# Row maxima of the scale chains in one VectorE operation with an accumulator, with another order of the work

## The chip, the core and the metric

The kernel runs on one core of a Trainium2 chip. Its engines work beside each other, each through its own stream of instructions in program order: TensorE multiplies matrices, VectorE, ScalarE and GpSimd work on elements, and DMA queues move data. An instruction that waits holds everything behind it on its engine. The metric is the device time of one execution in microseconds, the median of three runs.

## The reference

Three stages follow each other, in float32; the first weights arrive as float64.

```python
scores = scale * q @ k.T                      # 2 batches, 8 heads, 576 tokens, 64 wide
# heads 0-3: a local band of 32 positions; heads 4-7: every 32nd position
attn = exp(scores - max) / sum
x = attn @ v                                  # 1152 tokens x 512
h = maximum(maximum(x @ w1, x @ w2), x @ w3)  # 512 x 768 each
x2 = h @ w_out                                # 768 x 512
for e in range(4):                            # p: the normalised domain_probs
    out += p[:, e:e+1] * (maximum(x2 @ we1[e], 0) @ we2[e])
```

The experts are 512 x 1024 and 1024 x 512.

## The kernel before

**Split numbers.** Every product of the dense stages is made from fp16 pairs: an operand is scaled by a power of two, and split into hi (ScalarE, `split`) and lo (VectorE, the rest); three matmuls per piece give hi·hi + hi·lo + lo·hi (`mm3`, lines 350 to 352). The scale comes from a chain for each operand: a maximum per partition (VectorE `absmax`, line 132), or a bound by a sum (ScalarE `sum_bound`, line 129); if there are several, a reduction of them (line 95); a small matmul that lays all partitions' values beside each other in PSUM, `rows` (line 98); then on VectorE a maximum over these 128 columns (line 100), the guard and the factor (`m`, line 111, or line 119 for float64 words), a bit operation that keeps the exponent (line 114 or 122) and a reciprocal (`s`, line 105). There are 21 such chains: 4 for v, 6 for groups of w1 to w3, 1 for w_out, 2 for x2, and 4 each for the experts' two weight matrices.

**Tiling.** Tokens go in four groups i (two batches, halves of 256 and 320). Attention takes each group in four head pairs p, two local and two strided: scores and exponentials (`att_a`, the atom aa; score blocks are `sps`, lines 259 and 264, in two PSUM buffers; the exponentials are line 275), normalisation (an; the multiplication on GpSimd, line 298), transposition (at), product with v (ap, `ops`; the result is split into x, lines 344 and 345). The columns of w1 to w3 come in six groups fc of 128: load lw, maximum wa, decoding of float64 words wd (ScalarE lines 162 and 163, VectorE 166 and 167), split wp. `g1` (atom g) multiplies one token group by one column group for all three weights, into three PSUM tiles out of a pool of three; the first is copied out by ScalarE (line 396), the other two are joined by VectorE (397, 398). `g2` (atom go) multiplies by w_out into the same pool; ScalarE copies to `x2acc` (line 418) and VectorE takes the maximum. The experts' first product runs as seven products over sums and differences of blocks (lines 564 to 566), whose operands `prep_w1` (atom ew) and `x2_ops` (xw, yw) make; `gemm1` adds the products up on VectorE (572 to 579) and splits the hidden values (588 and 589, or 585 and 586 with GpSimd).

**Order.** The table ORDER lists the atoms of everything up to the first expert in the order in which the code issues them; XS, W20, W10, W2S and W1S say how many steps of the preparation for later products go between the experts' products. A scheduler then sets each engine's stream by its own model of time, so a moved atom changes more than its own place. In ORDER, oa, od, os and op are the maximum, decoding, scale and split of w_out; ew are steps of the first expert's weight preparation.

Of the kernel before, what the change touches and what calls it, by code (L numbers as in the profile page):

```python
# [8 lines left out]
F32 = mybir.dt.float32  # L9
# [5 lines left out]
ALU = mybir.AluOpType  # L15
# [14 lines left out]
QB = 3  # L30
XS = [0, 1, 1]
W20 = [2, 1, 3, 2, 0, 5, 1, 2]
W10 = [1, 1, 2, 2, 4, 4, 0, 3]
W2S = [0, 0, 1, 0, 1, 1, 4, 6, 3, 0, 7, 5, 7, 3, 1, 3, 1]
W1S = [8, 3, 1, 2, 0, 14, 6, 6, 4, 0, 4, 4, 0, 5, 0, 3, 3]

ORDER = """
    lq02 lq00 lq01 aa00 lw0 lv01 lq03 lv00 aa01 vs0 wa0 wd0 an00 lq20 at00 ap00 lw1 aa02 lv21 wp0 an01 at01
    ap01 an02 lq22 aa03 an03 at02 lv20 ap02 at03 lq21 lq23 ap03 aa20 vs2 lq10 aa21 wa1 an20 at20 wd1 ap20 lq12
    aa22 g00 lw3 an21 at21 aa23 ap21 wp1 an22 lw2 lv11 at22 ap22 an23 g01 at23 lv10 lq11 ap23 wd2 wa2 wa3 wd3  # L40
    wp3 aa11 wp2 g20 lq32 g21 lv30 an11 g03 aa10 g23 aa12 vs1 lw4 at11 ap11 an10 at10 ap10 lq30 wa4 wd4 lq13
    wp4 g04 g02 an12 lv31 aa13 at12 ap12 lw5 wa5 an13 at13 wd5 lq33 wp5 aa30 an30 ap13 lo0 lq31 aa33 aa31 vs3
    g22 lo1 g24 at30 ap30 an31 at31 an33 oa1 at33 ap31 ap33 aa32 an32 oa0 at32 g25 od0 od1 ap32 os op3 op0 g10
    op4 fo ew g05 op1 op2 ew ew op5 go20 ew go00 ew go23 ew ew g11 ew ew go22 ew g12 go21 ew go01 ew go03 ew
    go02 ew xw g15 xw g13 fw g14 ew xw xw g30 g31 xw g32 xw fw g33 ew xw xw ew xw g34 fw fw fw g35 cl go10 m
    go11 go30 fw m go13 fw go12 go31 go32 go33 m yw yw yw yw yw yw yw yw m yw fw
"""
# [6 lines left out]
def kernel(ctx, tc, qk0l, qk0s, qk1l, qk1s, vl, vs0, vs1, vn, masks, w123, wo, probs, we1, we2, out):  # L54
    nc = tc.nc
# [33 lines left out]

    def all_max(maxes, n):  # L90
        red, eye = maxes, ident if maxes.dtype == F32 else identb
        if n > 1:

            red, eye = sc.tile([128, 1], BF16, tag="red", name=nm("red")), identb
            nc.vector.tensor_reduce(red, maxes, AX.X if len(maxes.shape) == 2 else AX.XY, ALU.max)

        rows = rows_tile()
        nc.tensor.matmul(rows, red.to_broadcast([128, 128]), eye, start=True, stop=True)
        allr = sc.tile([128, 1], F32, tag="allr", name=nm("allr"))
        nc.vector.tensor_reduce(allr, rows, AX.X, ALU.max)  # L100
        return allr

# [5 lines left out]
    def scale_of(maxes, n, inv=None, f=0.25):  # L108

        m = sc.tile([128, 1], F32, tag="m", name=nm("m"))  # L110
        nc.vector.tensor_scalar(m, all_max(maxes, n), TINY, f, ALU.max, ALU.mult)
        if inv is None:
            inv = const.tile([128, 1], F32, name=nm("inv"))
        nc.vector.tensor_scalar(inv.bitcast(I32), m.bitcast(I32), 0x7F800000, None, ALU.bitwise_and)
        return finish_scale(inv)

    def scale_of64(maxes, n, inv=None):
        m = sc.tile([128, 1], F32, tag="m", name=nm("m"))
        nc.vector.tensor_scalar(m, all_max(maxes, n), REBIAS, TINY64, ALU.mult, ALU.max)
        if inv is None:  # L120
# [338 lines left out]
    def x2_ops(j, pool):  # L459
# [7 lines left out]
        (nc.gpsimd if j else nc.vector).tensor_tensor(t[2], a[0][0], a[1][0], ALU.subtract)  # L467
        nc.vector.tensor_tensor(t[3], a[0][1], t[1], ALU.subtract)
        yield
# [83 lines left out]
    def gemm1(e, j):  # L553
# [3 lines left out]
        for fp in range(4):  # L557
# [22 lines left out]
            for b in range(2):  # L580
                tok = slice(n * b, n * b + n)
                hi, lo = [hh[:, i, :, tok].rearrange("p (a f) t -> p a f t", f=4)[:, :, fp, :] for i in range(2)]
                if b and (e or j):
                    nc.scalar.activation(c[:, b], c[:, b], AF.Relu)
# [272 lines left out]
```

## Time and profile before

| | us |
|---|---|
| median of three runs (575.19 to 577.38) | 576.4 |
| the profiled execution | 576.38 |
| its span in the trace | 574.6 |
| TensorE busy (matmuls) | 551.3 |
| VectorE busy | 364.6 |
| ScalarE busy | 264.4 |
| GpSimd busy | 127.9 |

In the rows below the engines are PE (TensorE), PEld (its weight loads), DVE (VectorE), ACT (ScalarE) and POOL (GpSimd). A row gives the line of the kernel, the operation, and the tiles written and read; the brackets or the last column give the time for which the engine had been idle just before, and which engine's work ended that. The busy share over the whole span hides that the stages differ, so the windows come first.

### The profile page before, as it was taken

What the parts mean: (1) busy time and instruction counts of PE and PEld (TensorE: products, weight loads), DVE (VectorE), ACT (ScalarE), POOL (GpSimd) and SP (SyncE); (2) the same over time, 40 slices, a digit from 0 to 9 for tenths busy, and PEclk for the clock granted to TensorE, in tenths of its full rate; (3) what the DMA queues carried; (4) which work ended last, traced back from release to release, by engine and by line L of the source; (5) the groups of instructions that cost most, each with busy time, mean ns of one, the idle gap of its engine ahead of it and who ended that gap; (6) DMA issues with size and microseconds to landing.
All of it is one profiled execution on the core that took longest, in us unless ns stands there. A gap on an engine that the chain in (4) does not pass through costs nothing.

```text
span 574.6 us, 9788 instructions
## 1 busy us (share of the span) xinstructions
PE 551.3 (96%) x3944; PEld 373.6 (65%) x3944; DVE 364.6 (63%) x676; ACT 264.4 (46%) x559; POOL 127.9 (22%) x115
## 2 busy tenths in 40 slices
PE   5789699999999999899999999999999999999997
PEld 3668588887877777674447875446875446875443
DVE  3888999687652254988864765984764943765111
ACT  4678877586541132567826443605433611433000
POOL 1233554310111101023504211260211200221000
PEclk9588999999999999999999999999999999999999
DMA  8999636000400003004260000340000000000111
GB/s 291 337 352 306 206 115 256 2 2 2 147 1 1 1 2 141 6 1 148 73 220 0 1 2 1 128 165 1 2 1 1 1 0 1 2 1 0 56 55 56
DMA packets 16109, 44.33 MB, mean 77 GB/s; under 512 B 2280, under 2 KB 2280, under 8 KB 15296
## 3 DMA queue, kind: packets, MB, share of 16 engines
q1 hardware_dynamic: 15920, 43.41, 22.6%
q8 instruction: 31, 0.51, 0.4%
q10 hardware_dynamic: 144, 0.30, 0.1%
q14 instruction: 14, 0.11, 0.1%
HBM read 41.34 MB, written 2.36 MB: 76 GB/s over the span
## 4 chain that ended last, share of the span: by engine, by line
PE 77%; DVE 8%; DMA 6%; ACT 5%; issue 3%; POOL 1%; SPq 0%; ACTq 0%; DVEq 0%; POOLq 0%
PE e L350 11%; PE e L352 11%; PE e L351 11%; PE w L564 9%; PE w L566 9%; PE w L565 8%; PE g L350 6%; PE g L351 6%; PE g L352 6%; DMA v<-in_vl_dram 2%; DMA st<-in_w_dram 2%; ACT w L129 1%; PE ops L337 1%; DMA st<-in_we_dram 1%; ACT p L275 1%
## 5 line engine op out<-in xcount | busy, mean ns | idle before, releaser
L565 PE MATMUL w<-xops,w1ops 128*128 128x256 f16 (+1 forms) x448 | 128.0, 286 | 0.7 <-DVE xops L473 0.7
L564 PE MATMUL w<-xops,w1ops 128*128 128x256 f16 (+1 forms) x448 | 127.4, 286 | 1.0 <-DVE c L573 0.6
L566 PE MATMUL w<-xops,w1ops 128*128 128x256 f16 (+1 forms) x448 | 128.0, 286 | 0.0
L351 PE MATMUL g<-x,w 128*128 128x256 f16 (+1 forms) x288 | 82.4, 288 | 0.0
L350 PE MATMUL g<-x,w 128*128 128x256 f16 (+1 forms) x288 | 81.6, 289 | 0.2 <-ACT t L396 0.2
L352 PE MATMUL g<-x,w 128*128 128x256 f16 (+1 forms) x288 | 81.8, 286 | 0.0
L586 POOL TENSOR_TENSOR h<-c,h 128x640 f16<-128x640 f32 (+1 forms) x28 | 36.5, 1304 | 186.4 <-ACT h L585 182.1
L694 DVE SCALAR_TENSOR_TENSOR x2acc<-e,coef,x2acc 128x512 f32<-128x512 f32 x27 | 20.1, 747 | 69.5 <-PE e L352 69.5
L588 ACT ACTIVATE h<-c 128x512 f16<-128x512 f32 (+1 forms) x36 | 24.1, 676 | 83.0 <-DVE c L578 82.8
L351 PE MATMUL e<-st,h 128*128 128x512 f16 x144 | 54.6, 379 | 0.0
L352 PE MATMUL e<-w,h 128*128 128x512 f16 x144 | 54.6, 379 | 0.0
L350 PE MATMUL e<-st,h 128*128 128x512 f16 x144 | 54.6, 379 | 0.0
L352 PE MATMUL e<-st,h 128*128 128x512 f16 x144 | 54.6, 379 | 0.0
L351 PE MATMUL e<-w,h 128*128 128x512 f16 x144 | 54.4, 379 | 0.0
L350 PE MATMUL e<-w,h 128*128 128x512 f16 x144 | 54.0, 379 | 0.0
L565 PEld LDWEIGHTS <-w1ops 128*128 128x128 f16 x448 | 43.8, 98 | 13.4 <-issue 1.6
L566 PEld LDWEIGHTS <-w1ops 128*128 128x128 f16 x448 | 43.8, 98 | 12.6 <-issue 1.7
L564 PEld LDWEIGHTS <-w1ops 128*128 128x128 f16 x448 | 43.8, 98 | 12.0 <-DVE c L577 0.2
L352 PEld LDWEIGHTS <-h 128*128 128x128 f16 x288 | 28.2, 98 | 34.0
L350 PEld LDWEIGHTS <-h 128*128 128x128 f16 x288 | 28.2, 98 | 33.0
L351 PEld LDWEIGHTS <-h 128*128 128x128 f16 x288 | 28.2, 98 | 32.7
L400 POOL TENSOR_TENSOR h<-t,h 128x256 f16<-128x256 f32 (+1 forms) x24 | 21.9, 918 | 89.4 <-ACT h L399 89.4
(133 smaller groups left out, 1028.7 us busy)
## 6 DMA issues: line engine op xcount, KB each, us to landing
st<-in_we_dram SPq DMA_DIRECT2D x16, 1024.0 KB, 5.2
st<-in_w_dram SPq DMA_DIRECT2D x6, 1536.0 KB, 11.2
st<-in_wo_dram SPq DMA_DIRECT2D x2, 1536.0 KB, 8.4
qk<-in_qk1s_dram SPq DMA_DIRECT2D x4, 684.0 KB, 11.5
out_dram<-x2acc SPq DMA_DIRECT2D x8, 256.0 KB, 2.0
qk<-in_qk1l_dram SPq DMA_DIRECT2D x4, 496.0 KB, 11.3
qk<-in_qk0l_dram SPq DMA_DIRECT2D x4, 400.0 KB, 12.2
qk<-in_qk0s_dram SPq DMA_DIRECT2D x4, 384.0 KB, 12.9
```

Source lines behind the costliest of these rows:

```text
L129: nc.scalar.activation(junk, src, AF.Abs, scale=2.0**-12, accum_out=dst)
L275: nc.scalar.activation(p3[:, g, :], s3[:, j, :], AF.Exp, bias=ngm[:rows, g : g + 1], scale=0.125, accum_out=sm[:rows, g : g + 1],)
L350: nc.tensor.matmul(psum, lh, rh, start=i == 0, stop=False)
L351: nc.tensor.matmul(psum, lh, rl, start=False, stop=False)
L352: nc.tensor.matmul(psum, ll, rh, start=False, stop=i == n - 1)
L400: nc.gpsimd.tensor_tensor(hh[:, 1, fc, :], t1[:, :n], hh[:, 0, fc, :], ALU.subtract)
L564: nc.tensor.matmul(pt, wh, xh, start=k == 0, stop=False)
L565: nc.tensor.matmul(pt, wh, xl, start=False, stop=False)
L566: nc.tensor.matmul(pt, wl, xh, start=False, stop=k == 1)
L586: nc.gpsimd.tensor_tensor(lo, c[:, b], hi, ALU.subtract)
L588: nc.scalar.activation(hi, c[:, b], AF.Relu)
L694: nc.vector.scalar_tensor_tensor(acc[:, t, :], pt, coef[:, t : t + 1], acc[:, t, :], ALU.mult, ALU.add)
```

## The change

The maximum and the guard-and-factor become one `tensor_scalar` on the 128x128 `rows` in PSUM: each value is multiplied by the factor and held above the guard, written back in place, and the maximum over the columns goes to `m` through the accumulator. 42 VectorE instructions become 21. In `x2_ops` of the second halves one more subtraction runs on GpSimd; in the first expert's first `gemm1` two blocks of hidden values are split by ScalarE and GpSimd instead of ScalarE and VectorE. ORDER and the lists are other ones; of the parts of ORDER that moved, the diff shows two. The maximum of w_out (oa) comes after its decoding (od), and so by `sum_bound` on ScalarE instead of `absmax` on VectorE.

```diff
-XS = [0, 1, 1]
-W20 = [2, 1, 3, 2, 0, 5, 1, 2]
-W10 = [1, 1, 2, 2, 4, 4, 0, 3]
-W2S = [0, 0, 1, 0, 1, 1, 4, 6, 3, 0, 7, 5, 7, 3, 1, 3, 1]
-W1S = [8, 3, 1, 2, 0, 14, 6, 6, 4, 0, 4, 4, 0, 5, 0, 3, 3]
+XS = [0, 0, 8]
+W20 = [4, 1, 6, 0, 1, 1, 3, 3]
+W10 = [0, 2, 2, 2, 5, 2, 2, 3]
+W2S = [0, 1, 1, 0, 0, 0, 5, 7, 4, 0, 7, 3, 6, 2, 0, 3, 0]
+W1S = [10, 0, 1, 5, 0, 16, 5, 7, 4, 0, 2, 2, 0, 3, 1, 5, 0]
...
-    go02 ew xw g15 xw g13 fw g14 ew xw xw g30 g31 xw g32 xw fw g33 ew xw xw ew xw g34 fw fw fw g35 cl go10 m
+    ew g13 ew ew xw g30 ew g14 ew fw xw g32 g31 xw g33 g15 xw xw xw ew g34 g35 ew xw xw cl fw xw go30 go10
-    op4 fo ew g05 op1 op2 ew ew op5 go20 ew go00 ew go23 ew ew g11 ew ew go22 ew g12 go21 ew go01 ew go03 ew
+    ew op1 g05 op2 g10 op3 op5 go20 ew ew ew go00 ew go23 ew g11 go03 ew go22 ew g12 go21 go01 ew ew fw go02
...
@@ -87,7 +87,8 @@
         return f"{p}{uid[0]}"
 
 
-    def all_max(maxes, n):
+    def all_max(maxes, n, f, least):
+
         red, eye = maxes, ident if maxes.dtype == F32 else identb
         if n > 1:
 
@@ -96,9 +97,9 @@
 
         rows = rows_tile()
         nc.tensor.matmul(rows, red.to_broadcast([128, 128]), eye, start=True, stop=True)
-        allr = sc.tile([128, 1], F32, tag="allr", name=nm("allr"))
-        nc.vector.tensor_reduce(allr, rows, AX.X, ALU.max)
-        return allr
+        m = sc.tile([128, 1], F32, tag="m", name=nm("m"))
+        nc.vector.tensor_scalar(rows, rows, f, least, ALU.mult, ALU.max, accum_out=m)
+        return m
 
     def finish_scale(inv):
         s = const.tile([128, 1], F32, name=nm("s"))
@@ -107,16 +108,14 @@
 
     def scale_of(maxes, n, inv=None, f=0.25):
 
-        m = sc.tile([128, 1], F32, tag="m", name=nm("m"))
-        nc.vector.tensor_scalar(m, all_max(maxes, n), TINY, f, ALU.max, ALU.mult)
+        m = all_max(maxes, n, f, TINY)
         if inv is None:
             inv = const.tile([128, 1], F32, name=nm("inv"))
         nc.vector.tensor_scalar(inv.bitcast(I32), m.bitcast(I32), 0x7F800000, None, ALU.bitwise_and)
         return finish_scale(inv)
 
     def scale_of64(maxes, n, inv=None):
-        m = sc.tile([128, 1], F32, tag="m", name=nm("m"))
-        nc.vector.tensor_scalar(m, all_max(maxes, n), REBIAS, TINY64, ALU.mult, ALU.max)
+        m = all_max(maxes, n, REBIAS, TINY64)
         if inv is None:
             inv = const.tile([128, 1], F32, name=nm("inv"))
         nc.vector.tensor_scalar(
@@ -465,7 +464,7 @@
         nc.vector.tensor_tensor(t[0], a[1][0], a[1][1], ALU.add)
         nc.vector.tensor_tensor(t[1], t[0], a[0][0], ALU.subtract)
         (nc.gpsimd if j else nc.vector).tensor_tensor(t[2], a[0][0], a[1][0], ALU.subtract)
-        nc.vector.tensor_tensor(t[3], a[0][1], t[1], ALU.subtract)
+        (nc.gpsimd if j else nc.vector).tensor_tensor(t[3], a[0][1], t[1], ALU.subtract)
         yield
         for n, src in enumerate((t[1], a[0][0], a[0][1], t[2], t[0], t[3], a[1][1])):
             hi, lo = xops[j][:, n, 0], xops[j][:, n, 1]
@@ -580,7 +579,7 @@
             for b in range(2):
                 tok = slice(n * b, n * b + n)
                 hi, lo = [hh[:, i, :, tok].rearrange("p (a f) t -> p a f t", f=4)[:, :, fp, :] for i in range(2)]
-                if b and (e or j):
+                if b and (e or j or fp > 1):
                     nc.scalar.activation(c[:, b], c[:, b], AF.Relu)
                     nc.scalar.copy(hi, c[:, b])
                     nc.gpsimd.tensor_tensor(lo, c[:, b], hi, ALU.subtract)
```

ScalarE at the second column group (w123_1), before: the exponentials of p110, of a strided pair, stand behind the two decode steps (lines 162 and 163 of the next group).

```order
L275 ACTIVATE p96_447,asm99_450<-sps100_451,anm98_449 128x64 x4
L344 ACTIVATE x0_127<-ops60_323,s23_198 128x256
L136 ACTIVATE w123_1_242<-r93_431,s88_415 128x1536
L162 ACTIVATE st64_0_68<-st64_0_68 128x1536
L163 ACTIVATE st64_0_68<-st64_0_68 128x1536
L275 ACTIVATE p110_523,asm113_526<-sps114_527,anm112_525 128x64 x4
L344 ACTIVATE x0_127<-ops65_345,s23_198 128x256
L275 ACTIVATE p145_686,asm148_689<-sps149_690,anm147_688 128x96 x2
L312 COPY pt109_521<-tps108_516 96x512
```

After, the pair is called p98 (sps102), and line numbers are smaller by one:

```order
L274 ACTIVATE p89_426,asm92_429<-sps93_430,anm91_428 128x64 x4
L343 ACTIVATE x0_127<-ops55_312,s28_214 128x256
L135 ACTIVATE w123_1_243<-r88_423,s75_385 128x1536
L274 ACTIVATE p98_460,asm101_463<-sps102_464,anm100_462 128x64 x4
L161 ACTIVATE st64_0_68<-st64_0_68 128x1536
L162 ACTIVATE st64_0_68<-st64_0_68 128x1536
L343 ACTIVATE x0_127<-ops60_335,s28_214 128x256
L274 ACTIVATE p153_814,asm156_817<-sps157_818,anm155_816 128x96 x5
```

The four exponentials moved ahead of the decode steps; five of a local pair, p153 (before p145), run behind them.

TensorE round the chain of v of token group i = 1, before: `rows185` stands between the two score blocks sps224 and sps225 of one strided pair.

```order
L259 MATMUL sps224_1133<-mk_125,identb_108 120x324
L264 MATMUL sps224_1133<-qk208_1027 120x108 x3
L98 LDWEIGHTS red184_943
L98 MATMUL rows185_945<-identb_108,red184_943 128x128
L310 MATMUL tps189_956<-ident_103,p145_686 96x128 x3
...
L259 MATMUL sps225_1143<-mk_125,identb_108 120x324
L264 MATMUL sps225_1143<-qk208_1027 120x108 x3
```

After (`rows180`, blocks sps222 and sps223):

```order
L258 MATMUL sps223_1112<-mk_125,identb_108 120x324
L263 MATMUL sps223_1112<-qk211_1076 120x108 x3
L349 LDWEIGHTS w123_0_145
L349 MATMUL g1141_679<-x2_129,w123_0_145 128x256
...
L99 LDWEIGHTS red179_935
L99 MATMUL rows180_937<-identb_108,red179_935 128x128
L309 MATMUL tps184_945<-ident_103,p158_832 96x128 x3
```

The second score block moved ahead of the chain's matmul.

ScalarE at the splits of the first expert's weights, `w1ops`, before: the copies t1340 and t1351 of two g1 tiles stand round six splits.

```order
L396 COPY t1340_1859<-g1337_1820 128x320
L136 ACTIVATE w1ops333_1746<-st326_1692,s347_1898 128x1024 x2
L136 ACTIVATE w1ops333_1746<-st327_1694,s347_1898 128x1024
L136 ACTIVATE w1ops333_1746<-st64_0_68,s347_1898 128x1024
L136 ACTIVATE w1ops333_1746<-st64_1_69,s347_1898 128x1024
L136 ACTIVATE w1ops333_1746<-st327_1694,s347_1898 128x1024
L418 ACTIVATE x2acc_61<-g2341_1867,x2s_133 128x256
L396 COPY t1351_1939<-g1348_1900 128x320
L136 ACTIVATE w1ops333_1746<-st326_1692,s347_1898 128x1024
```

After, three copies of g2 tiles and then the six splits, with the copy of g1348 behind:

```order
L417 ACTIVATE x2acc_61<-g2337_1952,x2s_133 128x256
L417 ACTIVATE x2acc_61<-g2347_1990,x2s_133 128x256
L135 ACTIVATE w1ops323_1748<-st310_1622,s342_1982 128x1024 x2
L135 ACTIVATE w1ops323_1748<-st311_1624,s342_1982 128x1024
L135 ACTIVATE w1ops323_1748<-st64_0_68,s342_1982 128x1024
L135 ACTIVATE w1ops323_1748<-st64_1_69,s342_1982 128x1024
L135 ACTIVATE w1ops323_1748<-st311_1624,s342_1982 128x1024
L395 COPY t1351_2053<-g1348_2014 128x320
L135 ACTIVATE w1ops323_1748<-st310_1622,s342_1982 128x1024
L395 COPY t1361_2120<-g1358_2081 128x320
```

The splits moved to a later place among the g1 and g2 tiles: g2347 is the last tile copied out ahead of them, g1348 the first behind.

## Rows read from the trace of the kernel before

**Rows 1.** Busy time of each engine (us, instructions) in four stretches, granted TensorE clock, DMA

```profile
0.00:90.00 90.00, 72.70 (x637) 59.50 (x638) 73.70 (x144) 68.11 (x203) 37.19 (x49) 0.89 0.79 257
90.00:230.00 140.00, 139.78 (x1225) 110.55 (x1223) 80.09 (x153) 64.70 (x141) 21.15 (x27) 1.00 0.17 57
230.00:245.00 15.00, 13.36 (x99) 9.36 (x98) 14.84 (x34) 8.92 (x15) 0.00 (x0) 1.00 0.01 4
245.00:560.00 315.00, 314.94 (x1942) 189.57 (x1940) 193.71 (x346) 122.63 (x204) 69.61 (x40) 1.00 0.11 39
```

**Rows 2.** The same columns for two stretches of 10 us

```profile
40.00:50.00 10.00, 8.02 (x79) 6.74 (x77) 8.87 (x12) 8.49 (x28) 4.28 (x7) 0.83 1.03 321
...
60.00:70.00 10.00, 6.96 (x84) 5.99 (x82) 10.00 (x13) 8.45 (x22) 5.62 (x6) 1.00 0.53 163
```

**Rows 3.** Timeline of TensorE, 42 to 68 us: start, duration, instruction, idle before

```profile
42.37 0.36 PE L259 MATMUL sps<-mk,identb 128*128 128x480 bf16 x1 [1.99 <-ACT p L275]
...
44.94 1.12 PE L337 MATMUL ops<-pt,v 96*64 96x64 f32 x16
...
58.67 0.23 PE L98 MATMUL rows<-identb,red 128*128 128x128 bf16 x1 [1.30 <-DVE red L95]
...
61.40 0.68 PE L337 MATMUL ops<-pt,v 64*64 64x64 f32 x16 [0.69 <-DVE x L345]
...
67.88 0.30 PE L259 MATMUL sps<-mk,identb 128*120 128x324 bf16 x1 [2.04 <-ACT p L275]
```

**Rows 4.** Timeline of ScalarE at 39 us

```profile
39.52 1.63 ACT L163 ACTIVATE st<-st 128x1536 f32<-128x1536 f32 x1
```

**Rows 5.** Timeline of VectorE, 56 to 59 us

```profile
56.36 2.19 DVE L166 SCALAR_TENSOR_TENSOR st<-st 128x1536 int32<-128x1536 int32 x1
58.47 0.14 DVE L95 TENSOR_REDUCE red<-vm 128x1 bf16<-128x2 f32 x1
```

**Rows 6.** Instructions by line and shape: busy us, mean ns of one, idle before

```profile
L132 DVE TENSOR_REDUCE x2mx<-x2acc 128x1 f32<-128x256 f32 (+1 forms) x16 | 7.1, 450 | 16.4 <-ACT x2acc L418 16.3
...
L275 ACT ACTIVATION_READ_ACCUMULATOR p<-sps,anm 128x1 f32 (+1 forms) x76 | 17.0, 224 | 0.0
...
L100 DVE TENSOR_REDUCE allr<-rows 128x1 f32<-128x128 f32 x21 | 5.6, 280 | 5.9 <-PE rows L98 5.9
...
L111 DVE TENSOR_SCALAR m<-allr 128x1 f32<-128x1 f32 x15 | 2.2, 147 | 0.2
...
L467 POOL TENSOR_TENSOR st<-x2acc 128x640 f32<-128x640 f32 x1 | 1.5, 1539 | 19.6 <-ACT x2acc L418 19.6
```

**Rows 7.** Timeline of VectorE at 85 us

```profile
85.62 1.73 DVE L132 TENSOR_REDUCE mxo<-st 128x1 f32<-128x1536 f32 x1
```

**Rows 8.** Timeline of ScalarE, 133 to 142 us

```profile
133.93 0.42 ACT L396 COPY t<-g 128x320 f32<-128x320 f32 x1 [0.69 <-PE g L352]
134.89 6.34 ACT L136 ACTIVATE w1ops<-st,s 128x1024 f16<-128x1024 f32 x6 [0.53 <-DVE s L105]
```

**Rows 9.** Timeline of TensorE, 133 to 137 us

```profile
133.79 0.30 PE L350 MATMUL g<-x,w 128*128 128x320 f16 x1
...
136.91 0.30 PE L352 MATMUL g<-x,w 128*128 128x320 f16 x1
```

**Rows 10.** Timeline of VectorE, 228 to 242 us

```profile
228.69 0.82 DVE L468 TENSOR_TENSOR st<-x2acc,st 128x640 f32<-128x640 f32 x1
...
240.97 1.28 DVE L589 SCALAR_TENSOR_TENSOR h<-c,h 128x512 f16<-128x512 f32 x2
```

**Rows 11.** Timeline of GpSimd and VectorE, 10 to 29 us

```profile
10.78 0.82 POOL L298 TENSOR_TENSOR p<-p,ar 128x384 f32<-128x384 f32 x1 [0.29 <-DVE ar L297]
...
27.77 1.73 DVE L166 SCALAR_TENSOR_TENSOR st<-st 128x1536 int32<-128x1536 int32 x1
28.00 2.18 POOL L298 TENSOR_TENSOR p<-p,ar 128x384 f32<-128x384 f32 x1 [2.04 <-DVE ar L297]
```

More of the change, by code (lines that the diff above doesn't have):

```diff
@@ L30 @@
 QB = 3
-XS = [0, 1, 1]
-W20 = [2, 1, 3, 2, 0, 5, 1, 2]
-W10 = [1, 1, 2, 2, 4, 4, 0, 3]
-W2S = [0, 0, 1, 0, 1, 1, 4, 6, 3, 0, 7, 5, 7, 3, 1, 3, 1]
-W1S = [8, 3, 1, 2, 0, 14, 6, 6, 4, 0, 4, 4, 0, 5, 0, 3, 3]
-ORDER = """
[L38 to L43, printed above, removed]
-    op4 fo ew g05 op1 op2 ew ew op5 go20 ew go00 ew go23 ew ew g11 ew ew go22 ew g12 go21 ew go01 ew go03 ew
-    go02 ew xw g15 xw g13 fw g14 ew xw xw g30 g31 xw g32 xw fw g33 ew xw xw ew xw g34 fw fw fw g35 cl go10 m
-    go11 go30 fw m go13 fw go12 go31 go32 go33 m yw yw yw yw yw yw yw yw m yw fw
+XS = [0, 0, 8]
[3 more added lines that the diff above has]
+W1S = [10, 0, 1, 5, 0, 16, 5, 7, 4, 0, 2, 2, 0, 3, 1, 5, 0]
+ORDER = """
+    lq02 lq00 lq01 lw0 lv01 lq03 aa00 lv00 lq20 aa01 aa02 vs0 wa0 wd0 an00 at00 lw1 ap00 lv21 an01 at01 lv20
+    an02 aa03 ap01 wp0 at02 ap02 an03 at03 ap03 aa20 lw2 vs2 wa1 an20 at20 lq22 lq21 lq23 aa21 wd1 aa22 an22
+    lq10 ap20 aa23 an21 at21 ap21 wp1 at22 g00 an23 g01 at23 ap22 lv11 lq12 lw3 lv10 wa3 wd2 ap23 lq11 wa2 wd3
+    wp2 wp3 lq32 g20 g21 g03 aa11 aa10 lv30 an11 g23 an10 aa12 vs1 at10 at11 ap11 an12 lv31 at12 ap10 lw4 g02
+    lq30 wa4 wd4 lq13 wp4 lw5 lq33 wa5 wd5 aa13 aa30 wp5 ap12 lq31 an30 an13 at13 aa33 ap13 g04 aa31 vs3 g22
+    at30 g24 ap30 lo0 an31 lo1 at31 an33 at33 od0 ap31 ap33 aa32 an32 at32 g25 oa0 ap32 od1 oa1 os op0 fo op4
+    ew op1 g05 op2 g10 op3 op5 go20 ew ew ew go00 ew go23 ew g11 go03 ew go22 ew g12 go21 go01 ew ew fw go02
+    ew g13 ew ew xw g30 ew g14 ew fw xw g32 g31 xw g33 g15 xw xw xw ew g34 g35 ew xw xw cl fw xw go30 go10
+    go32 m go31 m go13 go11 go12 go33 fw m fw yw m yw yw yw yw yw yw yw fw fw yw fw
 """
```

## Prediction

> **What bounds the kernel now.** I read the windows by stage first, to see where TensorE is not busy (it is the engine that is busy longest in all of them). It is busy for 72.70 us of the first 90, for 139.78 of the next 140, for 13.36 of the 15 from 230 us, and for 314.94 of the 315 after those [rows 1]. So a change can win only in the opening 90 us (17.3 us idle) and round 240 us (1.64 us idle); elsewhere it can only lose, by making TensorE wait where it does not wait now. The finer windows say what holds it in the opening: between 60 and 70 us VectorE is busy for 10.00 us of 10 and TensorE for 6.96 [rows 2]. The timeline of TensorE then names the single waits. At 42.37 us it has waited 1.99 us for exponentials of ScalarE, at 58.67 it has waited 1.30 for a small VectorE reduction, at 61.40 0.69 for an x split, at 67.88 2.04 for exponentials [rows 3]. Behind each is an in-order queue: at 42.37 the exponentials stood behind a decode step of 1.63 us that began at 39.52 [rows 4]; at 58.67 the 0.14 us reduction stood behind a decode step of 2.19 us [rows 5].
>
> **The change, part by part.**
>
> The fused operation. Of each of the 21 scale chains one VectorE row goes: the maximum over 128 columns (280 ns) and the guard-and-factor (147 ns) become one row over the same 128 columns that also writes them back [rows 6]. The trace has no VectorE operation with an accumulator. If the sum comes for free, a chain gains 0.147 us. If the accumulator has to be read out in a step of its own, the nearest row is ScalarE's read of 224 ns, and a chain loses 224 − 147 = 0.077 us [rows 6]; if the write-back costs a second pass as well, another 0.28, so 0.36 us. Off the path this is worth nothing, as TensorE is full there. On it stand the chains of the crowded stretch between 40 and 90 us, four or five, so the ends are 5 × (−0.147) = −0.7 and 5 × 0.36 = +1.8 us. I take 0, between the two cheap cases, whose rows are the nearest. The removed link saves little more: VectorE works in program order, and the link that follows waits behind whatever long operation stands between.
>
> A rule that speaks against this edit: the Trainium skill, page "VectorE: DVE Perf Modes", section "Two Vector instructions with no wait between them", counts an operation that also writes out its accumulator as two instructions, the main one and an accumulator read. On ScalarE the trace agrees (the 224 ns rows); no run here shows it on VectorE. By the rule the sum would be 5 × 0.077 = 0.4 us later than mine, within the range.
>
> The opening, by the new order. On ScalarE the four exponentials of a strided pair (p98) now stand ahead of the decode step, as the excerpt of ScalarE's order shows, so the 1.99 us at 42.37 goes. But the strided score block of the next half token group follows sooner, and its buffer waits for the exponentials of the local block, five with their reads, that now run behind both decode steps. I expect a wait of about the same size one block later: 0, bounds −2.0 and +0.5. Further on, the order uses the third weight group ahead of the fifth, takes one score block more ahead of the reduction for which TensorE waits at 58.67 (the excerpt of TensorE), and moves the two operations that read the maximum of w_out (1.73 us each on VectorE, one of them ahead of a split of w [rows 7]) to ScalarE. The waits at 58.67, 61.40 and 67.88 add up to 4.03 us. The sum of VectorE's work up to each milestone hardly changes, and VectorE is full there, so not all of it can go: I take three quarters, −3.0 us, with ends −4.0 (all) and 0 (VectorE's own sum decides).
>
> A new wait, at the first expert product. Before, ScalarE copies out the tile of a first-layer group (133.93, 0.42 us) and then makes six splits of the first expert's weights in one piece of 6.34 us [rows 8]. TensorE does not wait: it has tiles to fill whose buffers VectorE frees, and the next one that ScalarE must free comes late enough. After, as the excerpt shows, the six splits stand directly behind the last copy of w_out's product g2347 and ahead of the copy of g1348. Let P be the end of g2347 on TensorE. Its copy to x2acc takes about as long as the copy at 133.93 (0.42), the row maximum on VectorE 0.45, and the scale's last link 0.15, as the small rows do [rows 6, 8]; the splits follow, so they begin at about P + 1.1 and end at P + 7.4, and the copy of g1348 ends at P + 7.9. TensorE meanwhile runs the three tiles of that group, 36 matmuls. The 320-column matmuls start 0.136 us apart (from 133.79 to 136.91 are 23 steps) [rows 9], so they end at P + 4.9. Three buffers hold three tiles, and the next tile waits for the copy of g1348: 7.9 − 4.9 = 3.0 us. The tile after it needs the copy of g1358, which ScalarE can make only once that tile is there (about 0.4 us), and one further tile waits for VectorE behind its lo splits (about 0.3). Together +3.7 us, ends 0 (if TensorE comes late enough) and +5.0. TensorE's clock may follow: after the 1.99 us at 42.37 matmuls ran slower (16 of 64 columns took 1.12 us at 44.94 against 0.68 at 61.40) and the window from 40 to 50 us has a granted clock of 0.83, between the levels of 1.2 and 2.4 GHz [rows 2, 3]; after the 2.04 at 67.88 the window stays at 1.00 [rows 2, 3]. I take +0.3, ends 0 and +2.0.
>
> The x operands of the second half (225 to 245 us). VectorE is busy for 14.84 of these 15 us, and TensorE idles for 1.64 [rows 1]. One subtraction of 0.82 us and two splits of a hidden block (1.28 for a pair) leave VectorE [rows 10], with one link of the chain: 2.2 us less in front of the operands. GpSimd does the like subtraction in 1.54 us [rows 6] and was idle there. The gain cannot exceed the idle time; I take −1.1, ends −1.6 and 0.
>
> Here too a rule speaks against it: GpSimd's 128x384 product took 0.82 us alone and 2.18 us at 28.00, beside a VectorE operation of two tensors from 27.77 [rows 11]. The Trainium skill, page "SBUF — State Buffer", section "Who interferes with whom", says that a VectorE instruction with two SBUF inputs contends with a GpSimd one that reads SBUF; the trace agrees with this pair. By the rule the moved subtraction would take up to 1.54 + 1.4 us, and the gain would shrink to about 0.4.
>
> From 245 us on TensorE's stream is the same and full (0.06 us idle), the experts' filler lists only move work beside it: 0. The tail is untouched.
>
> Sum, against the profiled execution of 576.38 us (the span of 574.6 and 1.8 around it; the median of the three runs is 576.40, so no correction): 576.38 + 0 − 3.0 + 3.7 + 0.3 − 1.1 = 576.3 us.
>
> **Rivals.** First, the new wait does not come: the copies that release the buffers are done in time, because the splits' scale is ready sooner than I set it or TensorE reaches the place late. For it speaks that the same splits cost TensorE nothing before [rows 8]; against it the order, in which nothing but the splits stands between the two copies. Then 576.38 − 3.0 − 1.1 = 572.3 us, and 571.3 with the whole 4.0 of the opening.
>
> Second, slower: the opening gives nothing, because VectorE's saturated stretch (10.00 of 10 us) is the bound and no long operation leaves it before the w splits, while the new wait stays with its low clock. The place is 60 to 80 us; it decides if the first matmuls of the fourth weight group start no sooner than now. Then 576.38 + 0 + 3.7 + 1.0 − 0.4 = 580.7 us.
>
> Third, the fused operation is dear (a second pass and a read, 0.36 us a chain): 576.3 + 1.8 = 578.1, with the chains that start each x stage (two more) 578.8.
>
> Fourth, the change does not do what it says: VectorE still shows two rows a chain, one of them an accumulator read. Its time is that of the cheap end, 576.7, and it goes with the forecast.
>
> **How the numbers follow.** The forecast has 0.45 (with the fourth rival in it), the first rival 0.30, the second 0.17, the third 0.08. About 0.5% (2.9 us) is what a measurement of this kernel can tell from no change, so faster means under 573.5 and slower over 579.3. The forecast's own range, with its bounds added as independent, is 573.3 to 579.3, hardly any of it beyond either line. Faster: nearly all of the first rival and a little of the forecast, 0.31. Slower: most of the second, a third of the third, a little of the forecast, 0.22. Same: the rest, 0.47. The range that should hold the time 8 times in 10 reaches to the whole gain of the opening without the new wait and to the second rival: 571.3 to 580.7.
>
> **What would show it.** The fused step: 21 rows of 128x128 on VectorE with about 0.3 us each, and whether a read row follows. The opening: no wait of TensorE at 58 and 67 us, and the window of the first 90 us holds some 3 us less idle time. The new wait: about 3 us on TensorE for a ScalarE copy, between 140 and 160 us, behind six splits. The x operands: less than 1 us idle between 230 and 245. I am wrong if TensorE has no wait of over 1 us between 100 and 230 us, if the first 90 us end later than before, or if TensorE waits anew beyond 245 us.

## The result, and the profile after

The changed kernel takes 585.53 us (median of 4 runs, 580.79 to 585.92) against 576.40 (also of 4): ratio 1.0127, 95% interval 1.0098 to 1.0156. The quotient of the two medians alone would be 1.0158; one of the four runs took 580.79. The change is slower by more than 0.5%, and above the range of the prediction. The profiled execution takes 585.92 us, its span is 584.1 against 574.6. Three executions of the experiments below (724, 1467 and 2016 us, one each of three variants) lie far outside all others and are in no ratio, though they count in the medians.

The windows by stage of the changed kernel, with the columns of [rows 1] (the granted clock is the third number from the right):

```profile
0.00:90.00 90.00, 73.64 (x599) 60.34 (x599) 70.91 (x142) 64.77 (x196) 33.19 (x47) 0.83 0.77 257
90.00:150.00 60.00, 60.00 (x604) 50.18 (x604) 35.80 (x65) 35.98 (x81) 14.72 (x16) 1.00 0.18 63
150.00:180.00 30.00, 26.60 (x202) 20.05 (x200) 22.50 (x39) 21.32 (x42) 4.74 (x6) 0.94 0.20 71
235.00:260.00 25.00, 22.84 (x181) 17.37 (x180) 23.45 (x50) 14.04 (x25) 5.27 (x4) 1.00 0.18 66
260.00:570.00 310.00, 309.94 (x1904) 185.79 (x1902) 189.61 (x338) 118.56 (x198) 66.68 (x39) 1.00 0.12 40
```

TensorE idles for 16.36 us in the first 90 (17.30 before), for 3.40 in the stretch from 150 to 180 (0.22 before), for 2.16 round 245 us (1.64 before), and for 0.06 in the rest. Over the whole span that is only 2.8 us more. The other 6.7 us of the 9.5 are in the busy time: the clock is 0.83 in the first 90 us (0.89 before) and 0.94 from 150 to 180 (1.00). I count what the clock takes as the sum, over windows of 2 us, of TensorE's busy time times one minus the granted clock: 8.0 us before, 14.4 after. Idle time plus this loss explains 9.2 of the 9.5 us.

The new wait is where it was forecast. TensorE, then ScalarE, of the changed kernel:

```profile
164.16 0.40 PE L349 MATMUL g<-x,w 128*128 128x320 f16 x1 [2.83 <-ACT t L395]
...
168.06 0.30 PE L349 MATMUL g<-x,w 128*128 128x320 f16 x1 [0.57 <-ACT t L395]
```

```profile
157.46 6.34 ACT L135 ACTIVATE w1ops<-st,s 128x1024 f16<-128x1024 f32 x6 [0.56 <-DVE s L106]
163.71 0.40 ACT L395 COPY t<-g 128x320 f32<-128x320 f32 x1
...
167.59 0.43 ACT L395 COPY t<-g 128x320 f32<-128x320 f32 x1 [2.42 <-PE g L351]
```

The six splits stand ahead of the copy at 163.71, for which TensorE has waited 2.83 us, and the next tile waits 0.57 us for the copy at 167.59. Behind the wait the granted clock falls from 2.4 to 1.2 GHz:

```profile
162.00:164.00 2.00, 0.00 (x0) 0.00 (x0) 2.00 (x5) 2.00 (x3) 0.00 (x0) 1.00 0.00 0
164.00:166.00 2.00, 1.84 (x8) 1.05 (x8) 2.00 (x3) 1.16 (x2) 0.00 (x0) 0.56 0.00 0
166.00:168.00 2.00, 1.49 (x6) 0.71 (x5) 2.00 (x5) 0.41 (x1) 0.00 (x0) 0.59 0.00 0
```

The windows from 164 to 168 us read 0.56 and 0.59, which takes 1.42 us; read over 0.4 us at a time, the clock is 0.50 from 164.4 to 167.6 us.

The opening has other waits than before [rows 3], and about as many:

```profile
45.31 0.49 PE L349 MATMUL g<-x,w 128*128 128x256 f16 x3 [1.58 <-ACT x L343]
...
46.90 0.30 PE L258 MATMUL sps<-mk,identb 128*120 128x324 bf16 x1 [1.11 <-ACT p L274]
...
63.09 0.42 PE L309 MATMUL tps<-ident,p 128*96 128x128 f32 x2 [0.62 <-ACT pt L311]
...
64.32 0.68 PE L336 MATMUL ops<-pt,v 64*64 64x64 f32 x16 [0.80 <-DVE x L344]
...
77.49 0.22 PE L99 MATMUL rows<-identb,mx 128*128 128x128 bf16 x1 [1.38 <-ACT pt L311]
```

ScalarE there:

```profile
41.50 0.32 ACT L274 ACTIVATE p<-sps,anm 128x64 f32<-128x64 f32 x1
...
41.79 1.62 ACT L161 ACTIVATE st<-st 128x1536 int32<-128x1536 uint16 x1
43.29 1.60 ACT L162 ACTIVATE st<-st 128x1536 f32<-128x1536 f32 x1
44.76 0.50 ACT L343 ACTIVATE x<-ops,s 128x256 f16<-128x256 f32 x1
```

The exponentials (the last of them at 41.50) do stand ahead of the two decode steps now. But the x split behind these (44.76) is what TensorE waits for at 45.31, and exponentials after it at 46.90: 1.58 + 1.11 us in place of 1.99.

The fused operation (mean ns of one behind the comma) answers to [rows 6]:

```profile
L101 DVE TENSOR_SCALAR_CACHE_REDUCE rows<-rows 128x128 f32<-128x128 f32 x21 | 6.0, 295 | 6.3 <-PE rows L99 6.3
...
L101 DVE DVE_READ_ACCUMULATOR rows<-rows 128x1 f32 x21 | 2.9, 139 | 0.0
```

It is two rows each time, of 295 and 139 ns, where there were two of 280 and 147: 42 rows as before, although the program has 21 instructions less. The fourth rival of the prediction came true.

Round 245 us, ScalarE, VectorE, GpSimd and TensorE of the changed kernel:

```profile
239.88 0.61 ACT L583 ACTIVATE c<-c 128x512 f32<-128x512 f32 x1
...
240.66 0.62 ACT L584 CAST h<-c 128x512 f16<-128x512 f32 x1
241.18 0.83 ACT L471 ACTIVATE xops<-st,s 128x640 f16<-128x640 f32 x1
```

```profile
240.62 0.16 DVE L106 RECIPROCAL s<-inv 128x1 f32<-128x1 f32 x1
...
248.47 1.77 DVE L472 SCALAR_TENSOR_TENSOR xops<-x2acc,s,xops 128x640 f16<-128x640 f32 x1
```

```profile
248.41 1.16 POOL L585 TENSOR_TENSOR h<-c,h 128x512 f16<-128x512 f32 x1 [5.84 <-ACT h L584]
```

```profile
251.30 0.30 PE L563 MATMUL w<-xops,w1ops 128*128 128x320 f16 x1 [1.85 <-DVE c L571]
```

The scale is ready at 240.78 (240.62 + 0.16). The first hi split of the x operands starts at 241.18, behind rows of a hidden block that GpSimd now finishes (lines 583 and 584); and the lo split at 248.47 takes 1.77 us, beside GpSimd's 1.16 us on that block. TensorE waits 1.85 us for VectorE.

### The profile page after: what moved, and what is told of

It reads as the page before. It is cut to its first block, busy times and chain, and to the rows that moved or that the text cites. A ratio compares the mean times of both kernels' runs of the same rounds, so it can differ in the third digit from the quotient of the medians.

```text
span 584.1 us, 9791 instructions
## 1 busy us (share of the span) xinstructions
PE 558.0 (96%) x3944; PEld 378.8 (65%) x3944; DVE 361.1 (62%) x671; ACT 267.2 (46%) x565; POOL 131.5 (23%) x118
## 4 chain that ended last, share of the span: by engine, by line
PE 83%; ACT 5%; DVE 4%; DMA 4%; issue 2%; POOL 1%; SPq 0%; ACTq 0%; DVEq 0%; POOLq 0%
PE e L350 10%; PE e L351 10%; PE e L349 10%; PE w L563 8%; PE w L564 8%; PE w L565 8%; PE g L350 7%; PE g L349 7%; PE g L351 7%; DMA st<-in_w_dram 3%; PE sps L263 2%; ACT p L274 2%; PE ops L336 1%; PE tps L309 1%; ACT w L128 1%
## 5 line engine op out<-in xcount | busy, mean ns | idle before, releaser
L349 PE MATMUL g<-x,w 128*128 128x256 f16 (+1 forms) x288 | 82.6, 292 | 5.0 <-ACT t L395 3.4
L350 PE MATMUL g<-x,w 128*128 128x256 f16 (+1 forms) x288 | 84.3, 294 | 0.0
L351 PE MATMUL g<-x,w 128*128 128x256 f16 (+1 forms) x288 | 83.7, 292 | 0.0
L585 POOL TENSOR_TENSOR h<-c,h 128x640 f16<-128x640 f32 (+1 forms) x30 | 38.6, 1287 | 176.5 <-ACT h L584 169.9
```

The costliest lines, as they stand in the source:

```text
L349: nc.tensor.matmul(psum, lh, rh, start=i == 0, stop=False)
L350: nc.tensor.matmul(psum, lh, rl, start=False, stop=False)
L351: nc.tensor.matmul(psum, ll, rh, start=False, stop=i == n - 1)
L585: nc.gpsimd.tensor_tensor(lo, c[:, b], hi, ALU.subtract)
```

## The experiments

Each was compared with the kernel before on the same chip. There the kernel before has a median of 577.2 to 578.2 us, so ratios are what is compared. There is one profile of each. For each the table gives TensorE's idle time in four stretches, and the matmul time lost to the clock, worked out as above (us):

```
                            idle: 0-38  38-100  150-185  230-262 | clock: 0-38  38-100  150-185
before                            9.96    7.32     0.22     1.64 |        6.35    1.63     0
changed                           9.96    6.40     3.40     2.16 |        7.91    5.03     1.42
changed again                     9.76    8.06     3.40     2.17 |        9.04    1.60     1.42
g13 ahead of go02                 8.46    7.43     1.18     2.17 |        6.98    4.87     0
wait filled (3.3 us more work)    8.55    7.89     0.57     2.16 |        8.15    3.30     0
moves undone                      7.82    8.62     3.40     1.75 |        8.63    0        1.45
both repairs                     10.96    8.51     0.95     1.75 |        8.23    0        0
only the new table                8.69    6.47     0.57     1.64 |        8.30    4.68     0
only the operations               8.91   12.73     1.22     2.16 |        6.78    4.78     0
opening filled                   10.37   10.69     0.16     1.63 |        5.47    1.70     0
accumulator alone                 9.53    6.57     0.76     1.64 |        7.62    4.75     0
unfused                           9.04    6.91     0.57     1.26 |        7.23    1.70     0
subtraction only                  9.96    7.40     0.97     1.78 |        7.61    3.18     0
before with subtraction           7.97    6.35     0.77     1.47 |        8.34    4.64     0
```

**The changed kernel again.** No edit.

> The changed kernel unchanged, as the measure for the three others on the same chip. Theory: 580 to 586 us, with four stretches of low clock behind waits (47, 65, 78 and 164 us) in a slow execution and three in one of 581. Rival: the spread is noise without a pattern in the clock.

583.94 us (583.47 to 585.72), ratio 1.0113 (1.0089 to 1.0136). Of the low clocks that I expected at 47, 65, 78 and 164 us only those at 47 and 164 are in this profile. So in the opening the same waits are followed by a low clock in one execution and not in another; the one at 164 us is there in each of the three profiles that have the wait of 2.83 us. Over 19 runs of before on this chip, time and mean clock go together: the six shortest (575.7 to 577.4 us) have 0.978 to 0.985, the eleven longest (578.2 to 580.2) 0.970 to 0.976 (correlation −0.79). On the two other chips the tie is looser (−0.30 over 23 runs, −0.62 over 29), so the clock accounts for a part of the spread only.

**The wait taken away.**

```diff
-... go21 go01 ew ew fw go02
-    ew g13 ew ew xw g30 ...
+... go21 go01 ew ew fw g13
+    go02 ew ew ew xw g30 ...
```

> The changed kernel with one edit in ORDER: the group g13 is issued ahead of go02 instead of behind it, so that ScalarE copies out the first tile of g13 before the six splits of the first expert's weights. My theory (a wait of TensorE costs its own length and then 1.7 us more, because the granted clock falls to half for about 3.4 us after it): the waits of 2.83 and 0.57 us at 161 to 168 us go or shrink below 1 us, no window between 150 and 180 us has a clock below 1.00, and the kernel is 4 to 5 us faster than the changed one. Rival (only the wait itself costs): 3 us faster, the clock falls somewhere else. Rival (slack further on gives it back): less than 1 us faster.

580.38 us, ratio 1.0036 (1.0016 to 1.0056), against 1.0113 (1.0089 to 1.0136) for the changed kernel: 3.6 us faster by the medians, 4.5 by the ratios, with streams that differ near this place and hardly elsewhere. The stretch has 1.18 us idle and no low clock:

```profile
150.00:180.00 30.00, 28.82 (x227) 21.88 (x225) 22.39 (x39) 20.11 (x38) 5.78 (x6) 1.00 0.21 71
```

By the table, moving the splits is worth 3.40 + 1.42 − 1.18 = 3.6 us: 1.2 us of waiting stayed, and the clock had cost 1.42 us and not the 1.7 of the theory. The runs cannot tell this from the 4 to 5 us that I expected.

**The wait filled with work.**

```diff
-            mm3(
-                pt[:, :n],
...
+            for _ in range(3 if (i, fc) == (1, 3) and wi == 2 else 1):
+                mm3(
+                    pt[:, :n],
...
```

> The changed kernel, with the 12 matmuls of the third tile of g13 done three times over (24 more, 3.3 us of work, same values), so that TensorE works where it waited 2.83 us at 161 us. Clock theory: no low clock between 150 and 180 us, and although TensorE does 3.3 us more work the kernel is 1 to 2 us faster than the changed one. Rival (the low clock there does not come from the wait): the same low clock, and the kernel is 0.4 us slower or the same.

582.86 us, ratio 1.0083 (1.0052 to 1.0114). TensorE does 24 matmuls of 0.136 us more and the kernel takes 1.1 us less than the changed one by the medians; the intervals overlap, so the windows decide:

```profile
162.00:164.00 2.00, 2.00 (x17) 1.44 (x16) 2.00 (x3) 1.25 (x2) 0.00 (x0) 1.00 0.00 0
164.00:166.00 2.00, 1.43 (x12) 0.91 (x10) 2.00 (x5) 0.42 (x1) 0.00 (x0) 1.00 0.00 0
166.00:168.00 2.00, 2.00 (x16) 1.43 (x15) 2.00 (x6) 0.57 (x2) 0.10 (x1) 1.00 0.73 176
```

They read 1.00 where the changed kernel has 0.56 and 0.59. The wait is what lowers the clock there; the rival falls. The table agrees: no kernel without the wait of 2.83 us loses anything to the clock between 150 and 185 us.

**The moves undone.**

```diff
-        (nc.gpsimd if j else nc.vector).tensor_tensor(t[3], a[0][1], t[1], ALU.subtract)
+        nc.vector.tensor_tensor(t[3], a[0][1], t[1], ALU.subtract)
...
-                if b and (e or j or fp > 1):
+                if b and (e or j):
```

> The changed kernel with the fourth subtraction of the second halves back on VectorE and the two blocks of hidden values back on the ScalarE and VectorE form; TensorE's order is the same. Theory (these moves save VectorE 2.1 us ahead of the second x operands, as I priced them): 1 to 2 us slower than the changed kernel, in the stretch of 240 to 255 us. Rival (the wait there is set by something else): within 0.5 us of it.

583.26 us, ratio 1.0088 (1.0065 to 1.0111), not to be told from the changed kernel. It is not slower, as I had expected it to be, and yet there is an effect in the trace: the idle time round 245 us falls from 2.17 to 1.75. ScalarE and VectorE:

```profile
235.89 1.15 ACT L587 ACTIVATE h<-c 128x512 f16<-128x512 f32 x2
236.95 0.81 ACT L471 ACTIVATE xops<-st,s 128x640 f16<-128x640 f32 x1
```

```profile
236.64 0.15 DVE L106 RECIPROCAL s<-inv 128x1 f32<-128x1 f32 x1
...
244.86 0.87 DVE L472 SCALAR_TENSOR_TENSOR xops<-x2acc,s,xops 128x640 f16<-128x640 f32 x1
```

The first hi split starts 0.31 us behind the scale's last row (236.64) instead of 0.56, the two rows of hidden values ahead of it are done by then, and no lo split is stretched (0.87). VectorE has 2 us more work, and TensorE waits less.

**Both repairs.** g13 ahead of go02, and the moves undone.

> The changed kernel with g13 issued ahead of go02, and with the two blocks of hidden values and the fourth subtraction back on VectorE. Theory (the new wait with its clock costs 4 us, and the moves lose 0.4 us because ScalarE's two extra rows stand ahead of the hi splits and GpSimd holds up a lo split): about 4 us faster than the changed kernel, 579 to 581 us; TensorE's idle time between 230 and 262 us about 1.75 us instead of 2.17, and what is left above the kernel before lies in the first 100 us. Rival (the moves help once TensorE comes earlier): slower than the kernel with g13 alone moved.

581.00 us, ratio 1.0044 (1.0019 to 1.0068): as with g13 alone. The idle time is 1.75 us as expected; 0.4 us is too little to show in the times. What is left above before is not in the two repaired places; in the profiles most of it is idle time of the first 100 us (19.47 us against 17.28), as expected.

**Only the subtraction on GpSimd.** g13 ahead of go02 and only the hidden blocks back (one profile).

> The changed kernel with g13 issued ahead of go02 and the two blocks of hidden values back on VectorE, but the fourth subtraction on GpSimd. Theory (it is the hidden blocks that lose, by two ScalarE rows ahead of the hi splits and by GpSimd beside a lo split; the subtraction is a gain of VectorE time): TensorE's idle time between 230 and 262 us below 1.75 us, which it is with both undone. Rival (the subtraction gains nothing, because ScalarE's hi splits set the pace): 1.7 to 1.8 us.

579.19 us in one run; 1.78 us idle round 245 us, with 1.75 where both moves are undone and 2.17 where neither is. The rival holds: the subtraction gains nothing there, and the hidden blocks are what lost the 0.4 us. By which of the two ways of the theory, the unfused kernel below shows.

**The subtraction in the kernel before.** The first line of the diff above, the other way round, in the kernel before.

> The kernel before with one edit: the fourth subtraction of the second halves on GpSimd; TensorE's order is the same. Theory: 0.3 to 0.8 us off the 1.64 us of idle time between 230 and 262 us, the rest as before; 0 to 0.2% faster, too little to be told from no change. Rival (nothing hangs on it): the idle time stays at 1.64 us.

576.96 us, ratio 0.9984 (0.9966 to 1.0002); idle time 1.47 instead of 1.64. A gain of 0.2 us in the trace, less than forecast and not measurable.

**Only the new table.** ORDER and the five lists of the changed kernel in the kernel before.

> The kernel before with ORDER and the lists of the changed one, and nothing else of it; the scheduler sets other streams for it than for the changed kernel, since its times for the scale chain differ. Theory (the table is what costs): slower than before by 0.5 to 1.2%, with waits of TensorE at other places than in the changed kernel. Rival (the fused operation or the moves cost): within 0.3% of before.

577.54 us, ratio 0.9998 (0.9978 to 1.0019). My theory falls: the table costs nothing by itself. The wait at 161 us is not there (0.57 us), although the atoms are in the order of the changed kernel. In the opening the long waits are there again:

```profile
42.98 0.36 PE L259 MATMUL sps<-mk,identb 128*128 128x480 bf16 x1 [1.98 <-ACT p L275]
...
58.81 0.23 PE L98 MATMUL rows<-identb,red 128*128 128x128 bf16 x1 [0.76 <-DVE red L95]
...
62.12 0.43 PE L259 MATMUL sps<-mk,identb 128*120 128x324 bf16 x1 [2.42 <-ACT p L275]
```

**Only the operations.** The fused operation and the moves with the table of before.

> The changed kernel with the ORDER and the lists of the kernel before: fused operation and moves without the new table. Theory (the fused operation is worth nothing by itself: 0.30 and 0.14 us against 0.28 and 0.15): what differs from before comes from the streams that the scheduler sets anew, and lies in TensorE's idle time of the first 100 us and round 145 us, with the x stage 0.4 us worse; between -0.3 and +1% of before. Rival (the fused operation is a gain that the table hides): faster than before by over 0.3%, with no more idle time of TensorE anywhere.

587.92 us, ratio 1.0170 (1.0140 to 1.0199), the slowest of all. TensorE idles for 12.73 us between 38 and 100 us, 3.44 of them in one new wait:

```profile
93.55 0.27 PE L349 MATMUL g<-x,w 128*128 128x256 f16 x1 [3.44 <-DVE t L396]
```

The theory named the idle time, but not its size: 1.7% lies outside the −0.3 to +1% that I expected. The rival falls.

**The accumulator alone.** Here the streams are those of before, row for row; only the operation differs.

```diff
-        nc.vector.tensor_reduce(allr, rows, AX.X, ALU.max)
+        nc.vector.tensor_scalar(rows, rows, 1.0, 0.0, ALU.mult, ALU.max, accum_out=allr)
```

> The kernel before with the maximum over the 128 columns taken by the accumulator form (times 1, not below 0, written back in place) instead of the reduction; the guard-and-factor stays a row of its own, and all streams are those of before, row for row. Theory (the operation itself costs what the reduction does: 0.295 and a read of 0.139 us that overlaps what follows, against 0.280): within 0.3% of before. Rival (the second row costs on the path): 1 to 2 us slower, with longer waits of TensorE at 20 and 58 us.

577.70 us, ratio 1.0000 (0.9981 to 1.0020).

```profile
L100 DVE TENSOR_SCALAR_CACHE_REDUCE rows<-rows 128x128 f32<-128x128 f32 x21 | 5.9, 297 | 5.5 <-PE rows L98 5.5
...
L100 DVE DVE_READ_ACCUMULATOR rows<-rows 128x1 f32 x21 | 2.9, 138 | 0.0
```

The operation has two rows, 0.297 and 0.138 us, and 21 of them cost nothing that can be measured.

**Unfused.** The changed kernel with `all_max`, `scale_of` and `scale_of64` of before; the table and both moves stay.

> The changed kernel with the maximum and the guard-and-factor as two operations again; the new table and the moves stay. Streams are those of the run with the new table alone, but for the moved blocks. Theory (the fused operation costs through the streams that the scheduler sets when a chain has one instruction less): 5 us faster than the changed kernel, within 0.4% of before, TensorE's idle time between 150 and 185 us 0.6 us and not 3.40, no low clock there. Rival (the moves made the wait at 161 us): 3.40 us of idle time stays.

576.08 us, ratio 0.9985 (0.9962 to 1.0007). Putting the fused operation back into two takes the whole loss away. ScalarE at the splits:

```profile
154.65 0.43 ACT L396 COPY t<-g 128x320 f32<-128x320 f32 x1 [1.21 <-PE g L352]
154.97 6.34 ACT L136 ACTIVATE w1ops<-st,s 128x1024 f16<-128x1024 f32 x6
```

The copy at 154.65 of a g1 tile stands ahead of the six splits, TensorE idles for 0.57 us, and the clock stays at 1.00. The rival (the moves) falls. Round 245 us the moves even lower the idle time here, to 1.26 us (1.64 with the table alone). VectorE, GpSimd and TensorE there:

```profile
240.51 0.87 DVE L473 SCALAR_TENSOR_TENSOR xops<-x2acc,s,xops 128x640 f16<-128x640 f32 x1
```

```profile
240.58 2.42 POOL L586 TENSOR_TENSOR h<-c,h 128x512 f16<-128x512 f32 x1 [5.98 <-DVE xops L473]
```

```profile
242.44 0.30 PE L564 MATMUL w<-xops,w1ops 128*128 128x320 f16 x1 [0.96 <-DVE c L572]
```

As in the changed kernel, ScalarE's rows of a hidden block stand ahead of the hi splits, and the last lo split begins 4.97 us behind TensorE's first product of the second half. But here it begins 0.07 us ahead of GpSimd's row and takes 0.87 us; in the changed kernel it begins 0.06 us behind it and takes 1.77. TensorE's wait is 0.96 us instead of 1.85, shorter by the same 0.9. So what the moves cost in the changed kernel is the stretched split, and not ScalarE's rows.

**The opening filled.**

```diff
-            nc.tensor.matmul(
-                st[:rows, : n * nk], identb[:, :rows], mrhs.rearrange("p g k -> p (g k)"), start=True, stop=False
-            )
+            for more in range({(2, 0): 0, (2, 1): 10}.get((i, p), 0), -1, -1):
+                nc.tensor.matmul(
+                    st[:rows, : n * nk], identb[:, :rows], mrhs.rearrange("p g k -> p (g k)"), start=True, stop=more > 0
+                )
```

> The kernel before, with the mask matmul of the second score block of the third token group done eleven times instead of once (same values), so that TensorE works for about 3 us in its wait for a load at 12 to 15 us. Streams beyond 20 us change somewhat, as the scheduler counts the work. Clock theory: the clock stays at 1.00 through 12 to 30 us, where it was 0.50, and the lost matmul time of the first 38 us falls from 6.4 to under 3 us; the kernel gains only what of it was on the path, 0 to 3 us, since loads and VectorE set much of that stretch. Rival: the clock falls at the same time as before.

582.45 us, ratio 1.0080 (1.0053 to 1.0108). TensorE, and the clock:

```profile
9.68 0.32 PE L260 MATMUL sps<-mk,identb 128*128 128x384 bf16 x1 [1.17 <-DVE anm L273]
11.06 3.58 PE L260 MATMUL sps<-mk,identb 128*128 128x384 bf16 x11 [1.06 <-ACT p L276]
```

```profile
10.00:12.00 2.00, 0.94 (x5) 0.53 (x4) 0.12 (x1) 2.00 (x15) 1.02 (x2) 0.80 1.06 217
12.00:14.00 2.00, 2.00 (x8) 0.94 (x7) 1.83 (x2) 1.84 (x4) 0.20 (x1) 0.50 1.04 241
16.00:18.00 2.00, 0.86 (x8) 0.72 (x8) 1.22 (x1) 0.00 (x0) 0.61 (x2) 1.00 0.99 415
18.00:20.00 2.00, 1.38 (x9) 1.10 (x7) 1.99 (x3) 0.00 (x0) 0.00 (x0) 0.51 0.98 353
```

The clock falls almost as soon as the added work begins at 11.06 us (0.75 from 11.0 to 11.4 us, 0.50 from there), so nearly all of that work runs at 1.2 GHz. It rises at 14.5 us and falls again at 18. In the kernel before it fell about 1 us later (10 to 12 us read 1.00, 12 to 14 us 0.59). The waits of 1.17 and 1.06 us ahead of the added work had come already, so the added work did not test what it was meant to test. The matmul time lost in the first 38 us is 5.47 us, not under 3. The kernel is slower, but its streams beyond 20 us are other ones and it idles for 10.69 us between 38 and 100 us, so its time says nothing of the clock. The experiment is inconclusive on what a high clock there would be worth.

## Why the prediction was wrong

**The opening, −3.0 us: this is the step that failed**, the largest error that can be put down to the change. "The waits at 58.67, 61.40 and 67.88 add up to 4.03 us ... I take three quarters." They went from their places [rows 3], and 1.58 + 1.11, 0.62 + 0.80 and 1.38 + 0.46 us came at others. Idle time from 0 to 100 us is 17.28 before, 16.36 and 17.82 in the two profiles of the changed kernel: −0.9 and +0.5. With what the clock took it is 25.3 before, and 29.3 and 28.5 after; the kernel with the accumulator alone, whose streams are those of before, has 28.5. So the opening gained nothing that can be told from before's own spread. The bound of 0 had its reason in the prediction (VectorE full, its sum unchanged), and the weight belonged there: between 60 and 80 us VectorE is busy for all 20 us before and after, and TensorE idles for 3.30 and 3.26 us. Before (its first half is in [rows 2]), then after:

```profile
70.00:80.00 10.00, 9.74 (x94) 8.72 (x89) 10.00 (x21) 8.94 (x30) 4.07 (x4) 1.00 0.22 85
```

```profile
60.00:70.00 10.00, 8.58 (x73) 7.51 (x71) 10.00 (x16) 8.15 (x22) 4.69 (x6) 0.83 0.43 110
70.00:80.00 10.00, 8.16 (x80) 6.99 (x79) 10.00 (x17) 7.22 (x24) 4.50 (x4) 0.94 0.36 145
```

That this sum is what decided is not shown, since three of the four waits there after the change (0.62, 1.38, 0.46) end with a row of ScalarE. I had even named the mechanism for one of the waits, "about the same size one block later", and should have asked it of each.

**The new wait, +3.7 us: right in its place in the streams, in mechanism and in size.** 2.83 + 0.57 us against 3.0 + 0.4 + 0.3; no wait for VectorE came, and it stands at 161 us, where I had written 140 to 160. Taking most of it away gave 3.6 us by the medians and 4.5 by the ratios, its clock included.

**The clock, +0.3 us: mis-sized.** Behind this wait it is 1.42 to 1.45 us in three profiles of three, within the bound of 2.0 but five times what I took. In the opening the changed kernel loses 12.9 and 10.6 us to the clock, before 8.0 in its one profile; but other kernels as fast as before lose as much there (13.0 with the new table alone, 12.4 with the accumulator alone), so only the part at 164 us is shown to be the change's. One profile of before, with a low clock once beyond 38 us, was too little to price it from.

**The x operands, −1.1 us: wrong in sign.** VectorE lost its work and TensorE waited 0.5 us more. I had weighed contention for the subtraction, and not for the hidden block that goes to GpSimd as well: the last lo split, 0.06 us behind GpSimd, takes 0.9 us longer and TensorE waits for it. Where it does not, in the unfused kernel, the moves gain 0.4 us (1.26 against 1.64), still less than 1.1. The rule on contention, in the Trainium skill, page "SBUF — State Buffer", section "Who interferes with whom", that I had weighed for the subtraction, agrees with the trace for the hidden block instead: a lo split of 0.87 us took 1.77 beside GpSimd's 1.16.

**The fused operation, 0: right for the operation, and yet the cause.** In unchanged streams the accumulator form costs 1.0000 of before (0.9981 to 1.0020). The page "VectorE: DVE Perf Modes" of the Trainium skill, section "Two Vector instructions with no wait between them", is borne out: each fused operation shows an accumulator read, of 139 ns. But a chain with one instruction less makes the scheduler set other streams, and that is where the loss comes from: the same table and moves without the fusion give 0.9985, with it 1.0113. The prediction put the new streams down to the table. For the forecast as such this made no difference, since the streams were read as they are; for the sentence on the cause it does.

**The sums.** With the terms as measured, 576.4 + 0 + 3.2 (idle time from 150 to 185 us) + 1.4 + 0.5 makes 581.5 us, 5.1 us above before. By the ratios the change costs 7.3 us (1.0127) and 6.5 us (1.0113): the 2.2 and 1.4 us that are left would have to lie in the first 100 us, where the two profiles show 4.0 and 3.2 us more of idle time and clock than the one profile of before. How much of that is the change's stays open. The second rival (580.7: nothing from the opening, the new wait with its clock) was the one that came nearest, and had 0.17; its own test, the start of the fourth weight group, was not read. The forecast's own range was also added up wrongly: its bounds, as independent, give some −4.4 and +4.3 us, so 571.9 to 580.6 and not 573.3 to 579.3. Of the signs named, the two rows of the fused step and the new wait came; 3 us less idle time in the first 90 us and less than 1 us round 240 us did not.

**Open.** Why the scheduler puts the splits elsewhere when a chain has one instruction less was not looked into. With the old table the fused operation was run only together with the moves, so the loss of 1.7% there is shown for both together. Whether the changed streams make low clocks in the opening likelier, or these runs had more of them by chance, is not shown. No kernel here is shown to be faster than before: the unfused one and the one with the subtraction have intervals that reach 1.

## What to carry to other kernels

Where a scheduler sets the streams, an edit of one small operation is an edit of all of them: test the operation in unchanged streams, and the streams without the operation, before either is blamed. A wait of TensorE that goes from one place need not be a gain: where the long row in front of its releaser was only moved, look for the next consumer behind it. When work goes from VectorE to GpSimd, look at which rows of VectorE it will run beside. And price a new wait of some 3 us in a stretch that was full with the low clock behind it, from rows like it.

## What the runs showed of the hardware

- A TensorE wait of 2.83 us in a stretch that had been full was followed by a granted clock of 0.50, the level of 1.2 GHz (0.56 and 0.59 over the two windows of 2 us in which it fell and rose). This came in three profiles of three, and cost 1.42 to 1.45 us of matmul time beside the wait's own length; with 3.3 us of repeated matmuls in it the clock stayed at 1.00. Behind the wait of 3.44 us of the kernel with only the operations it was 1.72 us. In the opening a wait of 1.38 us was followed by a low clock, and one of 1.75 at the same place in another execution was not.
- The VectorE operation with an accumulator on 128x128 in PSUM is a row of 295 ns and a read of 139 ns, and the next row starts together with the read (163.58 us for both in the changed kernel).
- A VectorE split (128x640, its source and hi both from SBUF) and a GpSimd subtraction that began within 0.1 us of each other: with GpSimd first by 0.06 us, VectorE took 1.77 us and GpSimd 1.16; with VectorE first by 0.07 us, VectorE took its usual 0.87 and GpSimd 2.42.
